# A gate sum moved from TensorE to VectorE, and linear-attention denominators computed as compact rows and spread through DRAM

## The chip, the cores and the metric

The kernel runs on one core of one Trainium2 chip. The metric is the device time in microseconds (us) of one execution, and the median of several executions is quoted. The profile's "span" is 1.5 to 2.2 us shorter than the time of the same execution, because it starts and ends with the recorded instructions.

Engines in the profile: PE is TensorE (matmuls), PEld its weight loads, DVE is VectorE, ACT is ScalarE, POOL is GpSimd, SP is SyncE, which issues most DMA transfers here.

## The reference, cut to what matters

The input x has 2048 tokens of 1024 channels; there are 32 heads of width 32; all is bf16. Branch a is linear attention with a positive feature map, branch b is dilated sliding-window attention, and a gate per token mixes them.

```python
def _A_ref(x, wqkv, wo):                       # linear attention
    ...                                        # q, k, v: [B, 32, 2048, 32]
    phi = lambda t: jnp.where(t > 0, t + 1, jnp.exp(t)) + 1e-6
    pq, pk = phi(q), phi(k)
    kv = jnp.einsum("bhsd,bhse->bhde", pk, v)
    z = jnp.einsum("bhsd->bhd", pk)
    num = jnp.einsum("bhqd,bhde->bhqe", pq, kv)
    den = jnp.einsum("bhqd,bhd->bhq", pq, z)[..., None] + 1e-6
    o = num / den
    return merge_heads(o) @ wo                 # (shortened)
...                                            # _B_ref: 8 keys per query, dilation 2
x = A_x
g = _sigmoid((x * gate_w).sum(-1, keepdims=True))
a = _A_ref(x, A_wqkv, A_wo)
b = _B_ref(x, B_wqkv, B_wo)
# result: the gated mix of a and b (g times a plus 1 - g times b)
```

Two small things in it matter here. The gate needs one sum of 1024 products per token. The denominator needs one number per head and token: 32 x 2048 numbers, each a dot product of length 32.

Of the kernel before, what the change touches and what calls it, by code (L numbers as in the profile page):

```python
# [6 lines left out]
ACT = mybir.ActivationFunctionType  # L7
ALU = mybir.AluOpType
AX = mybir.AxisListType
BF16 = mybir.dt.bfloat16  # L10
F32 = mybir.dt.float32
I32 = mybir.dt.int32

D = 1024
H = 32
# [1087 lines left out]
def build_kernel(nc, A_x, A_wqkv, A_wo, B_x, B_wqkv, B_wo, gate_w, out):  # L1103
# [10 lines left out]
    def SB(shape, dtype, name, at=None):  # L1114
        n = SZ[dtype]
        for d in shape[1:]:
            n *= d
        if at is None:
            at = base[0]
            base[0] += (n + 31) // 32 * 32  # L1120
        uid[0] += 1
        h = nc.alloc_sbuf_tensor_at("%s_%d" % (name, uid[0]), list(shape), dtype, offset=at)
        return Tile("S", h, at, list(shape), dtype)
# [32 lines left out]
    GT = [("M", 1, 2, None)]  # L1156
    gt_hbm = nc.dram_tensor("gt_hbm", [4, 512], F32)
# [16 lines left out]
    gw = SB([128, 8], BF16, "gw")  # L1174
# [3 lines left out]
    gwr = SB([128, 8, 32], BF16, "gwr")  # L1178
    kvbd = SB([128, 8, 128], BF16, "kvbd")
    zbd = SB([128, 8, 128], BF16, "zbd")  # L1180
# [9 lines left out]
    gts = SB([128, 512], F32, "gts", at=ph)  # L1190
# [8 lines left out]
    RAr = Ring([SB([128, 512], F32, "ra%d" % i, at=t.lo) for i, t in enumerate((Er.t[0], Er.t[1], Lr.t[0], vr.t[0]))])  # L1199
# [5 lines left out]
    az = Ring([SB([128, H, 33], BF16, "az%d" % i) for i in range(2)])  # L1205
    top_ = base[0]
    base[0] = ph
    osb = Ring([SB([128, 1024], BF16, "o%d" % i) for i in range(2)])
    pr = Ring([SB([128, 512], BF16, "p%d" % i) for i in range(4)])
# [14 lines left out]
    def plan(seen):  # L1224
# [25 lines left out]
        def C(eng, fn, cost, writes, reads=()):  # L1250
            return P.op(eng, fn, cost, reads=reads, writes=writes, prio=-1)
# [19 lines left out]
        C("pool", lambda e: e.memset(zbd[:], 0.0), 0.9, [zbd.all()])  # L1271
# [31 lines left out]
        def gw_load(e):  # L1303
            with nc.allow_non_contiguous_dma(reason="tiny gate_w transposed load"):
                return e.dma_start(gw[:, :], gate_w.rearrange("(dc p) -> p dc", p=128))

# [9 lines left out]
        P.op("sp", gw_load, 0.6, writes=[gw.all()], prio=20, chan="gw", lat=0.5)  # L1316
# [69 lines left out]
        P.op("dve", lambda e: e.tensor_copy(gwr[:, :, :], gw[:, :, None].to_broadcast([128, 8, 32])), 0.3, reads=[gw.all()], writes=[gwr.all()])  # L1386
        gbank = main.next()

        def gate_fn(e):
            last = None  # L1390
            for dc in range(8):
                for u in range(4):
                    last = e.matmul(gbank.ap()[32 * u:32 * u + 32, :], gwr[:, dc, :], xT[:, dc, u * 512:(u + 1) * 512], start=(dc == 0), stop=(dc == 7),  # L1393
                                    tile_position=(0, 32 * u), skip_group_check=True)
            return last
        P.op("pe", gate_fn, 1.75, mode="c", reads=[gwr.all(), xT.all()], writes=[gbank.iv], name="gate")
        P.op("act", lambda e: e.activation(gts[:, :], gbank.ap(), ACT.Exp, scale=-1.0), act(512), reads=[gbank.iv], writes=[gts.all()])
        P.op("sp", lambda e: e.dma_start(gt_hbm[:, :], gts[0:128:32, :]), 0.6, reads=[gts.all()], writes=[GT], chan="gto", lat=1.0)

        def gate_in(e):  # L1400
            with nc.allow_non_contiguous_dma(reason="2048 gates"):
                return e.dma_start(gt[:, :], gt_hbm.rearrange("u (k p) -> p (u k)", p=128))
        P.op("sp", gate_in, 0.6, reads=[GT], writes=[gt.all()], chan="gti", lat=6.0)
# [82 lines left out]
        def after(n, f, cols=False):  # L1486
            later.append((slot_n[0] + n, f, cols))
            later.sort(key=lambda x: x[0])
# [74 lines left out]
        for j in range(4):  # L1563
            sl = slice(32 * j, 32 * j + 32)
            P.op("dve", lambda e, sl=sl: e.tensor_copy(zbd[sl, :, sl], kva[sl, :, 32:33].to_broadcast([32, 8, 32])), dps(256), reads=[kva.all()], writes=[zbd.all()])
            P.op("dve", lambda e, sl=sl: e.tensor_copy(kvbd[sl, :, sl], kva[sl, :, 0:32]), 0.3, reads=[kva.all()], writes=[kvbd.all()])
# [23 lines left out]
        def numer(u, j):  # L1590
            bank = main.next()
            w, wr = w_cols(2, j)
            xs, xr = x_chunk(u)
            group(bank, w, xs, [wr, xr])
            tgt, c0 = pqn(u)
            dst, reg = tgt[:, j, c0:c0 + 512], tgt.part((j, j + 1), (c0, c0 + 512))
            if u == 0:
                p_, preg = dst, reg
            else:
                pt, _ = pr.next()  # L1600
                p_, preg = pt[:, :], pt.all()
            phi(bank, p_, preg, 8 * u + j)
            def over():
                db = main.next()
                P.op("pe", lambda e: e.matmul(db.ap(), zbd[:, j, :], p_, start=True, stop=True), mm(512), reads=[zbd.all(), preg], writes=[db.iv], name="den")  # L1605
                R, _ = RAr.next()
                P.op("act", lambda e: e.activation(R[:, :], db.ap(), ACT.Ln, bias=eps[:, :]), act(512), reads=[db.iv, eps.all()], writes=[R.all()])  # L1607
                P.op("act", lambda e: e.activation(R[:, :], R[:, :], ACT.Exp, scale=-1.0), act(512), reads=[R.all()], writes=[R.all()])  # L1608
                P.op("dve", lambda e: e.tensor_tensor(dst, p_, R[:, :], ALU.mult), 0.65, reads=[preg, R.all()], writes=[reg])
            after(6 if u == 0 else 2, over)  # L1610
# [21 lines left out]
        nums = [(u, j) for u in range(4) for j in range(8)]  # L1632
        outs = [(t, jh) for t in range(NT) for jh in range(2)]
        for n, (u, j) in enumerate(nums):
            numer(u, j)
            slot(0)
            if n == 1:
                turn()
            if 3 <= n < 11:
                fold(n - 3, 0)  # L1640
                fold(n - 3, 1)
            if n >= 17:
                a_out(*outs.pop(0))
                slot(0)
        while later:
            slot(0)
        P.op("dve", lambda e: e.tensor_reduce(mx4[:, 2:3], qe[:, :], AX.X, ALU.max), 0.2, reads=[qe.all()], writes=[mx4.part((2, 3))], prio=1e5)
        while outs:
            a_out(*outs.pop(0))


        P.op("dve", lambda e: e.tensor_scalar(mx4[:, 1:2], mx4[:, 1:2], -1.0, None, op0=ALU.mult), 0.1, reads=[mx4.part((1, 2))], writes=[mx4.part((1, 2))], prio=1e5)

        def mx_out(e):
            with nc.allow_non_contiguous_dma(reason="512 maxima"):
                return e.dma_start(mx_hbm.rearrange("i p -> p i"), mx4[:, :])
        P.op("sp", mx_out, 0.6, reads=[mx4.all()], writes=[MX], chan="mxo", lat=8.0, prio=1e5)
        P.op("sp", lambda e: e.dma_start(mxr[0:1, :, :], mx_hbm[None, :, :]), 0.1, reads=[MX], writes=[mxr.all()], chan="mxi", lat=2.0, prio=1e5)
        P.op("dve", lambda e: e.tensor_reduce(mx1[:, :], mxr[:, :, :], AX.X, ALU.max), dps(512), reads=[mxr.all()], writes=[mx1.all()], prio=1e5)
        small = [mx1.all()]  # L1660
        P.op("dve", lambda e: e.tensor_scalar(mx1[:, 2:3], mx1[:, 2:3], 2.0, None, op0=ALU.max), 0.1, reads=small, writes=small, prio=1e5)
        for o, i0, i1 in ((ALU.max, 0, 1), (ALU.mult, 0, 0), (ALU.mult, 2, 3)):
            P.op("dve", lambda e, o=o, i0=i0, i1=i1: e.tensor_tensor(mx1[:, i0:i0 + 1], mx1[:, i0:i0 + 1], mx1[:, i1:i1 + 1], o), 0.1, reads=small, writes=small, prio=1e5)
        P.op("dve", lambda e: e.tensor_scalar(mx1[:, 0:1], mx1[:, 0:1], 40.0 / DH, None, op0=ALU.is_le), 0.1, reads=small, writes=small, prio=1e5)
        P.op("dve", lambda e: e.tensor_scalar(mx1[:, 2:3], mx1[:, 2:3], 1e18 / (4 * DH), None, op0=ALU.is_le), 0.1, reads=small, writes=small, prio=1e5)
        flag_op = P.op("dve", lambda e: e.tensor_tensor(flag[:, :], mx1[:, 0:1], mx1[:, 2:3], ALU.mult), 0.1, reads=small, writes=[flag.all()], prio=1e5)


        for t in range(NT):
# [4 lines left out]
            for f0, f1 in parts:  # L1674
# [13 lines left out]
                if t == NT - 1 or f1 == 1024:  # L1688
                    c = f0 if t == NT - 1 else 0
                    P.op("sp", lambda e, e_=e_, r=r, o_=o_, c=c, f1=f1: e.dma_start(out2[e_, r * 128:(r + 1) * 128, c:f1], o_[:, c:f1]), 0.5,  # L1690
                         reads=[o_.part((c, f1))], chan="out%d_%d" % (os_, c), lat=1.0)

# [65 lines left out]
```

## The kernel before: the parts that the change and the argument touch

The kernel records its operations with their reads, writes and an assumed cost, and a small scheduler of its own lays them out for each engine and places the semaphore waits (`P.op(engine, function, assumed us, reads, writes)`). The order of each engine's list is fixed when the program is built. An instruction behind a wait comes after it.

The gate is a matmul with a one-column weight. The column is repeated 32 times, so that a 512-token chunk fills one of four column tiles. The result comes out as rows and takes a round trip through DRAM to become columns (one value per partition).

```python
P.op("dve", lambda e: e.tensor_copy(gwr[:, :, :], gw[:, :, None].to_broadcast([128, 8, 32])), ...)
def gate_fn(e):
    for dc in range(8):
        for u in range(4):
            last = e.matmul(gbank.ap()[32 * u:32 * u + 32, :], gwr[:, dc, :], xT[:, dc, u * 512:(u + 1) * 512],
                            start=(dc == 0), stop=(dc == 7), tile_position=(0, 32 * u), ...)
    return last
P.op("pe", gate_fn, 1.75, ...)
... # Exp on ScalarE, to DRAM as rows, back as columns
```

The denominators take one full matmul for each group of four heads and 512 tokens. `zbd` is block diagonal with z repeated over 32 columns, so the matmul computes each denominator 32 times, once for each of the 32 rows of its head. That is what lets the division follow without any spreading.

```python
def numer(u, j):              # u: chunk of 512 tokens, j: group of four heads
    ...                       # eight matmuls, then phi on ScalarE and VectorE -> p_
    def over():
        db = main.next()
        P.op("pe", lambda e: e.matmul(db.ap(), zbd[:, j, :], p_, start=True, stop=True), mm(512), ...)
        R, _ = RAr.next()
        P.op("act", lambda e: e.activation(R[:, :], db.ap(), ACT.Ln, bias=eps[:, :]), ...)
        P.op("act", lambda e: e.activation(R[:, :], R[:, :], ACT.Exp, scale=-1.0), ...)
        P.op("dve", lambda e: e.tensor_tensor(dst, p_, R[:, :], ALU.mult), 0.65, ...)
    after(6 if u == 0 else 2, over)
```

`after(n, f)` puts f behind n further slots. A slot is one work group of matmuls.

## Time and profile before

| | before |
|---|---|
| time, median of 3 (range) | 501.64 us (501.62 to 503.03) |
| TensorE busy | 493.2 us, 99% of the span |
| VectorE, ScalarE busy | 54%, 38% |
| gate matmuls on TensorE | 32 in 1.85 us |
| denominator matmuls on TensorE | 32, 0.216 us each, 6.9 us |
| from the end of the last computation to the end of the span | 3.9 us |

The first lines of the profile page of the kernel before give the span and each engine's busy time, its share of the span and its instructions. The third line is from the page's part on the chain that ended last: shares of the span by engine.

```profile
span 500.1 us, 11359 instructions
...
PE 493.2 (99%) x5113; PEld 231.4 (46%) x5113; DVE 267.6 (54%) x460; ACT 191.4 (38%) x331; POOL 6.6 (1%) x30
...
PE 96%; SPq 2%; DMA 1%; ACT 1%; issue 0%; DVE 0%
```

TensorE is almost never without work: its busy time (99%) and its share of the chain (96%) are the whole span but for the start and the end. Only work or waits taken from TensorE can shorten this kernel.

The groups of instructions of the kernel before, by form. The columns are: line, engine, operation, output from input, sizes, count | busy us in all, mean ns of one | idle time just before, and what ended it.

```profile
L1393 PE MATMUL ps_all<-xT,gwr 128*32 128x512 bf16 x32 | 1.9, 380 | 0.0
L1605 PE MATMUL ps_all<-p,zbd 128*128 128x512 bf16 x24 | 8.9, 379 | 0.0
L1605 PE MATMUL ps_all<-pq,zbd 128*128 128x512 bf16 x8 | 3.0, 379 | 0.0
L1607 ACT ACTIVATE ra<-ps_all,eps 128x512 f32<-128x512 f32 x32 | 21.5, 689 | 2.1 <-PE ps_all L1605 2.0
L1608 ACT ACTIVATE ra<-ra 128x512 f32<-128x512 f32 x32 | 19.9, 639 | 0.5
```

The mean of 379 ns is from the start of a matmul to its end in the record. It isn't what the matmul costs, because the next one starts 0.216 us after it, so the records overlap. The cost is read from the chain, in which matmuls follow each other. The chain of the kernel before, in order of time; the columns are start us, duration us, engine, tile, line, and count:

```profile
62.08 1.84 PE ps_all L1393 x32
...
342.17 0.23 PE ps_all L1605
342.42 0.69 ACT ra L1607
...
344.20 1.17 ACT ra L1607 x2
345.42 1.90 PE ps_all L1325 x8
...
412.71 27.63 PE ps_all L1325 x128
...
495.65 0.48 DVE o L1684
```

A full matmul costs 27.63 / 128 = 0.216 us, and a gate matmul on a quarter of the columns 1.84 / 32 = 0.058 us. At 342 the chain leaves TensorE for ScalarE: the Ln and Exp of the denominators had fallen behind, and TensorE lost about 0.4 us there. The last computation ends at 495.65 + 0.48 = 496.13.

Two readings of the kernel before. The first is the timeline at the first block of attention scores. The second is a window: stretch, its length, then busy time of TensorE, weight loads, VectorE, ScalarE and GpSimd, each with its count, then the granted clock, the share of DMA, and GB/s.

```profile
127.85 0.70 PE L1428 MATMUL ps_all<-qT,kT 32*64 32x57 bf16 x64
```

```profile
64.00:128.00 64.00, 64.00 (x328) 28.91 (x327) 34.57 (x57) 11.32 (x19) 0.00 (x0) 1.00 0.17 47
```

The gate and everything before attention lie ahead of the first of these, the denominators behind it.

### The profile page before, as it was taken

What the parts mean: (1) busy time and instruction counts of PE and PEld (TensorE: products, weight loads), DVE (VectorE), ACT (ScalarE), POOL (GpSimd) and SP (SyncE); (2) the same over time, 40 slices, a digit from 0 to 9 for tenths busy, and PEclk for the clock granted to TensorE, in tenths of its full rate; (3) what the DMA queues carried; (4) which work ended last, traced back from release to release, by engine and by line L of the source; (5) the groups of instructions that cost most, each with busy time, mean ns of one, the idle gap of its engine ahead of it and who ended that gap; (6) DMA issues with size and microseconds to landing.
All of it is one profiled execution on the core that took longest, in us unless ns stands there. A gap on an engine that the chain in (4) does not pass through costs nothing.

```text
span 500.1 us, 11359 instructions
## 1 busy us (share of the span) xinstructions
PE 493.2 (99%) x5113; PEld 231.4 (46%) x5113; DVE 267.6 (54%) x460; ACT 191.4 (38%) x331; POOL 6.6 (1%) x30
## 2 busy tenths in 40 slices
PE   8999999999999999999999999999999999999996
PEld 3444444444444445554545454444444444444443
DVE  3112136555676785665556564678776663234443
ACT  1111111111334345656655555489955543200000
POOL 5000000000000000000000000000000000000000
PEclk9999999999999999999999999999999999999999
DMA  8999990000023151011010000500000000011222
GB/s 230 202 209 312 344 283 1 1 0 1 12 90 125 32 182 34 24 42 26 27 43 24 24 1 3 171 0 1 0 2 0 1 1 0 3 43 64 84 85 67
DMA packets 47410, 34.91 MB, mean 70 GB/s; under 512 B 22261, under 2 KB 43125, under 8 KB 47354
## 3 DMA queue, kind: packets, MB, share of 16 engines
q1 hardware_dynamic: 46810, 33.59, 23.6%
q8 instruction: 42, 0.69, 0.6%
q10 hardware_dynamic: 544, 0.52, 0.4%
q14 instruction: 14, 0.11, 0.1%
HBM read 21.51 MB, written 8.40 MB: 60 GB/s over the span
## 4 chain that ended last, share of the span: by engine, by line
PE 96%; SPq 2%; DMA 1%; ACT 1%; issue 0%; DVE 0%
PE ps_all L1325 76%; PE ps_all L1680 11%; PE ps_all L1428 2%; PE ps_all L1447 2%; PE ps_all L1605 1%; SPq L1295 1%; PE ps_all L1526 1%; DMA w<-in_B_wqkv_dram 1%; PE ps_all L1454 1%; PE ps_all L1583 1%; SPq L1300 1%; ACT ra L1607 0%; PE ps_all L1393 0%; ACT e L1334 0%; ACT ra L1608 0%
## 5 line engine op out<-in xcount | busy, mean ns | idle before, releaser
L1325 PE MATMUL ps_all<-w,xT 128*128 128x512 bf16 x960 | 214.2, 379 | 1.1 <-DMA xT<-in_A_x_dram 0.9
L1325 PE MATMUL ps_all<-xT,w 128*128 128x512 bf16 x768 | 172.1, 379 | 0.1
L1325 PEld LDWEIGHTS ps_all<-w,xT 128*128 128x128 bf16 x960 | 91.1, 98 | 109.9 <-DMA w<-in_B_wqkv_dram 1.4
L1325 PEld LDWEIGHTS ps_all<-xT,w 128*128 128x128 bf16 x768 | 74.1, 98 | 88.8 <-ACT ra L1607 0.6
L1680 PE MATMUL ps_all<-w,qT 128*128 128x512 bf16 (+1 forms) x264 | 55.4, 373 | 0.0
L1680 PEld LDWEIGHTS ps_all<-w,qT 128*128 128x128 bf16 x264 | 25.8, 98 | 29.7
L1336 DVE TENSOR_SCALAR e<-e 128x512 bf16<-128x512 bf16 x64 | 18.4, 291 | 30.9 <-ACT e L1332 17.1
L1434 ACT ACTIVATE E<-ps_all 128x1824 bf16<-128x1824 f32 (+1 forms) x18 | 30.4, 1688 | 11.7 <-PE ps_all L1428 10.9
L1356 DVE CAST vst<-ps_all 128x512 bf16<-128x512 f32 x15 | 10.4, 692 | 42.7 <-PE ps_all L1325 42.7
L1437 DVE TENSOR_TENSOR E<-E,msk 128x1824 bf16<-128x1824 bf16 (+1 forms) x18 | 19.8, 1102 | 22.2 <-ACT E L1434 22.2
L1684 DVE SCALAR_TENSOR_TENSOR o<-ps_all,gm,xT 128x512 bf16<-128x512 f32 (+1 forms) x25 | 18.2, 729 | 23.0 <-PE ps_all L1680 22.8
L1334 ACT ACTIVATE e<-ps_all 128x512 bf16<-128x512 f32 x32 | 19.2, 601 | 27.5 <-PE ps_all L1325 26.0
L1332 ACT ACTIVATE e<-ps_all 128x512 bf16<-128x512 f32 x32 | 19.1, 598 | 26.7 <-PE ps_all L1325 25.8
L1281 DVE TENSOR_TENSOR mx<-mx,qT 128x1024 bf16<-128x1024 bf16 x32 | 20.7, 688 | 15.3 <-ACT qT L1360 15.2
L1281 DVE TENSOR_TENSOR mx<-mx,kT 128x1024 bf16<-128x1024 bf16 x32 | 20.7, 688 | 14.8 <-ACT kT L1357 14.7
L1357 ACT ACTIVATE vst<-ps_all 128x512 bf16<-128x512 f32 x17 | 10.2, 597 | 47.8 <-PE ps_all L1325 47.8
L1466 DVE TENSOR_TENSOR qT<-ps_all,L 128x456 bf16<-128x456 f32 (+1 forms) x36 | 21.0, 627 | 6.2 <-ACT L L1464 5.0
L1463 ACT ACTIVATE L<-ps_all 128x456 f32<-128x456 f32 (+1 forms) x36 | 17.8, 547 | 12.4 <-PE ps_all L1447 12.4
L1607 ACT ACTIVATE ra<-ps_all,eps 128x512 f32<-128x512 f32 x32 | 21.5, 689 | 2.1 <-PE ps_all L1605 2.0
L1338 DVE SCALAR_TENSOR_TENSOR pk<-ps_all,e 128x512 bf16<-128x512 f32 x32 | 21.9, 688 | 0.7
L1359 DVE TENSOR_SCALAR xT<-ps_all,g 128x512 bf16<-128x512 f32 x15 | 11.2, 750 | 19.9 <-PE ps_all L1325 19.9
L1360 ACT ACTIVATE qT<-ps_all 128x512 bf16<-128x512 f32 x14 | 8.4, 597 | 34.4 <-PE ps_all L1325 34.4
(77 smaller groups left out, 321.2 us busy)
## 6 DMA issues: line engine op xcount, KB each, us to landing
w<-in_A_wqkv_dram SPq DMA_DIRECT2D x6, 1024.0 KB, 7.0
v<-vB_hbm SPq DMA_DIRECT2D x36, 128.0 KB, 2.6
vB_hbm<-vst SPq DMA_DIRECT2D x32, 128.0 KB, 4.7
w<-in_B_wqkv_dram SPq DMA_DIRECT2D x4, 1024.0 KB, 8.4
out_dram<-o SPq DMA_DIRECT2D x15, 256.0 KB, 2.0
w<-in_A_wo_dram SPq DMA_DIRECT2D x2, 1024.0 KB, 5.2
w<-in_B_wo_dram SPq DMA_DIRECT2D x2, 1024.0 KB, 6.7
w<-in_B_wqkv_dram SPq DMA_DIRECT2D x6, 256.0 KB, 4.3
```

Source lines behind the costliest of these rows:

```text
L1281: P.op("dve", lambda e, m=m, op=op: e.tensor_tensor(m[:, 0:n], m[:, 0:n], src, op), 0.08 + n / 1920.0, reads=[m.all(), reg], writes=[m.all()],
L1325: last = e.matmul(bank.ap(), lhs(dc), rhs(dc), start=(dc == 0), stop=(dc == 7))
L1332: P.op("act", lambda e: e.activation(e_[:, :], bank.ap(), ACT.Exp), act(512), reads=[bank.iv], writes=[e_.all()])
L1334: P.op("act", lambda e: e.activation(e_[:, :], bank.ap(), ACT.Exp, accum_out=qe[:, col:col + 1]), act(512) + 0.1, reads=[bank.iv], writes= ...
L1336: P.op("dve", lambda e: e.tensor_scalar(e_[:, :], e_[:, :], 1.0, 1e-6, op0=ALU.min, op1=ALU.add), 0.25, reads=[e_.all()], writes=[e_.all()])
L1338: P.op("dve", lambda e: e.scalar_tensor_tensor(out=dst, in0=bank.ap(), scalar=0.0, in1=e_[:, :], op0=ALU.max, op1=ALU.add), dps(512), read ...
L1434: P.op("act", lambda e: e.activation(E[:, 0:32 * nq].rearrange("p (j q) -> p j q", j=4), ps[:, 4:8, 0:8 * nq], ACT.Exp), act(32 * nq), rea ...
L1437: P.op("dve", lambda e: e.tensor_tensor(ev(), ev(), m[:, :, :].rearrange("p r q -> p (r q)")[:, None, :].to_broadcast([128, 16, 2 * nq]), ...
L1466: P.op("dve", lambda e, L=L, h=h, q0=q0: e.tensor_tensor(qT[:, :, q0:q0 + nq], SO[h].ap(0, n).rearrange("p (c q) -> p c q", c=8), L[:, 0:n ...
L1607: P.op("act", lambda e: e.activation(R[:, :], db.ap(), ACT.Ln, bias=eps[:, :]), act(512), reads=[db.iv, eps.all()], writes=[R.all()])
L1680: last = e.matmul(bank.ap(0, f1 - f0), qT[:, dc, t * 128:(t + 1) * 128], ws[3][:, dc, f0:f1], start=(dc == 0), stop=(dc == 7))
L1684: P.op("dve", lambda e, bank=bank, o_=o_, t=t, n=n, i0=i0, i1=i1, tgt=tgt, c0=c0: e.scalar_tensor_tensor(out=o_[:, i0 * 128:i1 * 128].rear ...
```

## The change

The intent is to take both small things from TensorE. The gate is summed on VectorE: rows of x (tokens on partitions) are loaded once more, and one instruction multiplies them by a broadcast `gate_w` and sums along the row. The result is already a column. The denominators are computed once each and not 32 times: eight matmuls on column tiles give 32 rows for 512 tokens. Ln and Exp then run on one tile per 512 tokens instead of eight. The price is that each row must be spread over 32 partitions. That is done by storing the rows in DRAM in four copies, and loading each of these eight times.

```diff
-    zbd = SB([128, 8, 128], BF16, "zbd")
+    zsel = SB([128, 8, 32], BF16, "zsel")
-    RAr = Ring([... "ra%d" ... 4 tiles])
+    RAr = Ring([... "ra%d" ... 2 tiles])
+    RBr = Ring([SB([128, 512], F32, "rb%d" % i, at=kT.lo + 2048 * i) for i in range(12)])
+    xn = Ring([SB([128, 1024], BF16, "xn%d" % i, at=az.t[i].lo) for i in range(2)])
 ... # the gate
-        P.op("pe", gate_fn, 1.75, mode="c", ...)
-        P.op("act", ... Exp of [128, 512]); store to DRAM; load as columns
+        for t in range(NT):                                  # 16 tiles of 128 tokens
+            xt, xs_ = xn.next()
+            P.op("sp", lambda e, t=t, xt=xt: e.dma_start(xt[:, :], x2[...]), ..., chan="xn%d" % xs_)
+            P.op("dve", lambda e, t=t, xt=xt: e.scalar_tensor_tensor(out=xt[:, :], in0=xt[:, :], scalar=1.0,
+                 in1=gwb[:, :], op0=ALU.mult, op1=ALU.mult, accum_out=gt[:, t:t + 1]), dps(1024), ...)
+        P.op("act", ... Exp of gt [128, 16])
 ... # the denominators
+        def over(u):
+            db = main.next()
+            def fn(e):
+                for q in range(2):
+                    for c in range(4):
+                        last = e.matmul(db.ap()[32 * c:32 * c + 32, :], zsel[:, 2 * c + q, :],
+                                        tgt[:, 2 * c + q, c0:c0 + 512], start=(q == 0), stop=(q == 1),
+                                        tile_position=(0, 32 * c), skip_group_check=True)
+                return last
+            P.op("pe", fn, 0.55, mode="c", ...)
+            R, rs = RAr.next()
+            P.op("act", ... Ln, bias=eps);  P.op("act", ... Exp, scale=-1.0)
+            for c in range(4):
+                P.op("sp", ... e.dma_start(rc_hbm[u, 8 * c:8 * c + 8, :, :],
+                     R[32 * c:32 * c + 8, None, :].to_broadcast([8, 4, 512])), ..., chan="rco%d_%d" % (rs, c))
+            for j in range(8):
+                B, bs = RBr.next()
+                src = rc_hbm[u, 4 * j:4 * j + 4, :, :].rearrange("r k n -> (r k) n")[:, None, :].to_broadcast([16, 8, 512])
+                P.op("sp", ... e.dma_start(B[:, :], src), ..., chan="rci%d" % bs)
+                P.op("dve", lambda e, B=B, dst=dst: e.tensor_tensor(dst, dst, B[:, :], ALU.mult), 0.65, ...)
 ... # the order of work
             numer(u, j)
+            if j == 7:
+                after(3, lambda u=u: over(u))
             slot(0)
-            if n >= 17:
+            if n >= 20:
                 a_out(*outs.pop(0))
                 slot(0)
 ... # and three of the final output tiles now stand before the last eight a_out groups
```

Each new `chan` name is a further DMA channel.

## The prediction

> **What bounds the kernel now.** TensorE. The busy table has PE at 493.2 of 500.1 us (99%), VectorE 54%, ScalarE 38%. The chain of waits is 96% PE outside 10 us at the start (DMA) and 4 us at the end. In the chain the 128x512 matmuls follow each other every 0.216 us (128 in 27.63 us), at a granted clock of 1.0. So only issue slots or waits taken from PE can shorten it.
>
> **Removed from PE.** The 32 gate matmuls on four column tiles: 62.01 to 63.86 us in the timeline, 1.85 us. The 32 full-width denominator matmuls, 0.216 us each in the chain: 6.9 us.
>
> **Added to PE.** Four denominator blocks of 8 matmuls on column tiles. The gate block is the same form: 32 in 1.85 us, eight passes of 0.216 plus about 0.12 to switch. [...] So a new block is 2 x 0.216 + 0.12 = 0.55 us (estimate), four 2.2. Net: 6.9 + 1.85 - 2.2 = 6.55 us.
>
> **A wait that goes.** Between 342 and 345.5 us PE loses about 0.4 us to ScalarE, behind with Ln and Exp of the reciprocals (timeline). ScalarE loses 56 of 64 such passes, about 34 us, so it should vanish.
>
> **Moved or added elsewhere.** VectorE gets 16 products of 128x1024 with a sum; the trace has no such form, an estimate from the 128x512 form (0.69 us) is 1.2 to 1.3 us, 20 us in all. Fourteen lie between about 70 and 125 us, where VectorE is busy 34.6 of 64 us; it goes to about 80%, while PE has four banks of 1.73 us. DMA gets 4 MB of x rows, 1 MB of reciprocals written and 8 MB read. One block's spread is an estimate of 12 us: ScalarE 1.3, four stores and eight loads at about 0.5 us of issue each, two landings of about 2.5 us (v loads land in 2.6). [...] The instruction order puts ten groups or more between a block and its first reader on PE, so it is hidden. The first 62 us have DMA saturated (share 1.03), but the extra 0.75 MB there delays only loads needed later.
>
> **Predicted:** 501.64 - 6.55 - 0.4, plus 0.2 for small new waits: **494.9 us**, range 492.0 to 498.5. Faster by over 2%: 0.12; within 2%: 0.85; slower by over 2%: 0.03.
>
> **What would show it.** PE busy falls by about 7 us. The four denominator blocks take 0.5 to 0.6 us each on the chain. ScalarE busy falls from 191 to about 157 us, VectorE rises from 268 to about 287. VectorE is near 80% busy at 64 to 128 us; the chain there stays PE. Any wait of VectorE for reciprocals is under 3 us and PE doesn't notice.
>
> **What would make it wrong.** The summed product taking about 2 us, or VectorE waiting for each pair of x rows: evictions between 70 and 125 us then hold PE. A spread of over 17 us: VectorE, in order, then holds evictions in the numerator stage. The transposition of the state, one group earlier, waiting up to 1 us. A larger gain needs the removed PE work to cost more than its issue slots.

The sum: 501.64 - 6.55 - 0.4 + 0.2 = 494.9. The 0.55 us of a new block rests on the gate block alone, and the 2.5 us of a landing on the loads of v, with a median of 2.6 us on the page of the kernel before.

## More of the kernel before

The end of the program matters too. The kernel assumes that certain maxima are small, writes a flag, and behind the fast program stands a general path that the flag can choose. SyncE first waits for the last value of every DMA channel that the fast program used. Then every engine compares the flag, and normally takes a branch over the general path.

```python
def tail(e, eng):
    reg = e.alloc_register("fast_ok")
    e.wait_ge(*flag_op.val)
    e.reg_load(reg, flag[0:1, 0:1])
    if eng == "sp":
        for s, v in P.final:          # one entry for each DMA channel
            e.wait_ge(s, v)
    with e.If_eq(reg, 0):
        ...                           # general path
```

## The result, and the profile after

| | before | after |
|---|---|---|
| time, median of 4 (range) | 501.63 us (501.51 to 503.03) | 497.66 us (496.50 to 497.96) |
| ratio after / before, with 95% interval | | 0.991 [0.9887, 0.9934] |

The result is 4.0 us faster. The four executions of the kernel after lie 1.5 us apart, and the one that was profiled (497.96) is the slowest of them. A ratio, here and below, is the mean time of one kernel's runs over that of the other's runs of the same rounds, so it isn't quite the ratio of the medians quoted. The range of the prediction held, but the gain is 4.0 us where 6.7 were predicted. The rest of this document is about the missing 2.8 us.

The first lines of the profile page of the kernel after, and its chain by engine:

```profile
span 495.8 us, 11299 instructions
...
PE 479.6 (97%) x5016; PEld 228.4 (46%) x5081; DVE 275.9 (56%) x483; ACT 166.6 (34%) x287; POOL 6.3 (1%) x30
...
PE 89%; DMA 5%; issue 2%; SPq 2%; DVE 1%; ACT 1%; ACTq 0%
```

One trap comes first. TensorE's busy time seems to fall by 13.6 us, twice what was predicted. But this trace has 5016 matmuls against 5081 weight loads, where before both were 5113. The weight loads fall by exactly the 32 of the gate, so 65 matmul records are simply missing, and they leave false gaps. The waits of TensorE in the kernel after (us in all, times, longest) show it in their first line:

```profile
PE ps_all L1319 <- issue: 5.9, 37, 0.2
...
PE ps_all L1591 <- DVE xT L1332: 0.9, 1, 0.9
```

Thirty-seven gaps of 0.16 us that nothing released, inside stages that take no longer than before, are missing records. The second line is a real wait: once, for 0.9 us, TensorE stood before a denominator block (L1591), waiting for VectorE.

The groups of the kernel after that stand where those of the kernel before stood:

```profile
L1383 DVE SCALAR_TENSOR_TENSOR xn<-xn,gwb 128x1024 bf16<-128x1024 bf16 x16 | 18.9, 1221 | 0.0
L1383 DVE DVE_READ_ACCUMULATOR xn<-xn,gwb 128x1 f32 x16 | 1.4, 85 | 0.0
L1591 PE MATMUL ps_all<-xT,zsel 128*32 128x512 bf16 x24 | 1.8, 384 | 0.9 <-DVE xT L1332 0.9
L1591 PE MATMUL ps_all<-pq,zsel 128*32 128x512 bf16 x8 | 0.6, 384 | 0.0
L1607 DVE TENSOR_TENSOR xT<-xT,rb 128x512 bf16<-128x512 bf16 x24 | 16.4, 690 | 8.0 <-DMA rb<-rc_hbm 7.7
L1596 ACT ACTIVATE ra<-ps_all,eps 128x512 f32<-128x512 f32 x4 | 2.7, 684 | 4.2 <-PE ps_all L1591 4.2
```

The work is what was costed. A summed product takes 1.22 us and a read of the accumulator 0.085 us more. (The two groups of 16 show that each summed product is two instructions on VectorE.) The denominators take 2.4 us of TensorE in place of 6.9. ScalarE does Ln four times in place of 32. (The 6.9 is the cost on the chain. The busy time of 8.9 + 3.0 us in the groups of the kernel before counts each matmul to the end of its record.)

The same two readings of the first part as before, from the timeline and the windows of the kernel after:

```profile
125.66 0.70 PE L1411 MATMUL ps_all<-qT,kT 32*64 32x57 bf16 x64
```

```profile
62.00:126.00 64.00, 63.68 (x335) 29.01 (x339) 48.01 (x82) 13.50 (x24) 0.48 (x2) 1.00 0.40 127
```

The attention begins 2.19 us earlier. VectorE is busy 48.0 of 64 us in the stage that now holds the sums, not 34.6, and TensorE doesn't notice.

The chain of the kernel after, in order of time, around the denominators and at the end. The DMA issues below it give output from input, queue, kind, count, KB each, and median us from issue to landing.

```profile
339.07 3.38 DMA rc_hbm<-ra
...
346.81 6.43 DMA rb<-rc_hbm
353.26 0.69 DVE pq L1607
...
358.14 3.31 DMA rc_hbm<-ra
...
365.42 5.84 DMA rb<-rc_hbm
371.27 0.69 DVE xT L1607
371.97 0.61 DVE xT L1332
372.62 0.62 PE ps_all L1591 x8
373.24 6.15 PE ps_all L1319 x28
...
489.74 0.48 DVE o L1644
```

```profile
rb<-rc_hbm SPq DMA_DIRECT2D x32, 256.0 KB, 5.2
...
xn<-in_A_x_dram SPq DMA_DIRECT2D x16, 256.0 KB, 2.7
out_dram<-o SPq DMA_DIRECT2D x15, 256.0 KB, 2.1
```

This chain is the wait of 0.9 us, read backwards. The third denominator block starts at 372.62, because the phi of its last input on VectorE (L1332) ran at 371.97. That phi stood in VectorE's order behind a multiplication by reciprocals (L1607), and this multiplication waited for a load from DRAM which had been on its way since 365.42. The loads of x, 256 KB each and issued by SyncE, have a median of 2.7 us from issue to landing, and the outputs one of 2.1. The loads of reciprocals have the same size and a median of 5.2. But they come eight in a row: they were issued 0.7 us apart and landed about 1.0 us apart (the first of a row after 3.7 to 3.9 us, the last after up to 6.4), and in the midst of a row the DMA engines were fully busy, as this window of the kernel after shows (the share of DMA is the last but one number, 1.00):

```profile
346.00:350.00 4.00, 3.95 (x20) 1.80 (x19) 2.99 (x6) 1.38 (x4) 0.00 (x0) 1.00 1.00 264
```

A median of 5.2 us instead of the predicted 2.5 is where the wait begins.

Where the time went, stage by stage, from these records:

| stretch of the profiled runs | before | after | gain | predicted |
|---|---|---|---|---|
| start to first block of attention scores | 127.85 | 125.66 | 2.19 | 1.85 |
| from there to the end of the last VectorE operation | 368.28 | 364.57 | 3.71 | 5.1 |
| from there to the end of the span | 3.94 | 5.56 | -1.62 | 0 |
| sum | 500.07 | 495.79 | 4.28 | 6.75 (net of 0.2) |

(5.1 is 6.9 - 2.2 + 0.4.) About 1.4 us are missing in the middle and 1.6 us at the very end, where the change has edited nothing.

The last stretch holds no computation, so the page says little about it. The records of SyncE in the trace were read one by one for the following table; it isn't a view of the profile page. "Walk" is from the end of SyncE's last issue of an output to its branch over the general path: it contains a load of the flag (0.5 us) and the waits for all DMA channels. "Gap" is from the branch to SyncE's next instruction, which stands behind the general path.

| | SyncE instructions up to the branch | wait instructions in the walk | walk, us | gap, us | last VectorE operation to end of span, us |
|---|---|---|---|---|---|
| before | 157 | 26 | 2.21 | 0.51 | 3.94 |
| after | 229 | 36 | 3.25 | 1.08 | 5.56 |

The 53 DMA channels before have become 73, chiefly through the new rings (`rco`, `rci`, `xn`). One wait instruction carries up to two waits (each of the 36 records of the kernel after has two semaphores). So ten more wait instructions stand in the walk, which is 1.0 us longer, and the gap behind it is 0.6 us longer. By the same records the last output had landed 0.2 us before the branch in the kernel before, but 1.55 us before it in the kernel after: there SyncE is no longer waiting for data. Wait instructions follow each other every 0.061 us, so ten more are 0.6 us. Most of the other 0.4 us is one pause between two waits (0.40 us from the one to the next). It stands between SyncE's 207th and 208th instruction in all four kernels with the new denominators and 36 waits, whichever wait that is. Its cause is open.

The windows of the kernel after also say that the clock is not part of it. It is 1.00 up to 490 us, and its mean of 0.996 comes from the last slices alone, with no matmul in them. One of them:

```profile
492.00:494.00 2.00, 0.00 (x0) 0.00 (x0) 0.00 (x0) 0.00 (x0) 0.00 (x0) 0.50 0.08 19
```

### The profile page after: what moved, and what is told of

Read it like the earlier page. It is cut to its first block, busy times and chain, and to the rows that moved or that the text cites. A ratio compares the mean times of both kernels' runs of the same rounds, so it can differ in the third digit from the quotient of the medians.

```text
span 495.8 us, 11299 instructions
## 1 busy us (share of the span) xinstructions
PE 479.6 (97%) x5016; PEld 228.4 (46%) x5081; DVE 275.9 (56%) x483; ACT 166.6 (34%) x287; POOL 6.3 (1%) x30
## 4 chain that ended last, share of the span: by engine, by line
PE 89%; DMA 5%; issue 2%; SPq 2%; DVE 1%; ACT 1%; ACTq 0%
PE ps_all L1319 71%; PE ps_all L1640 11%; DMA rb<-rc_hbm 2%; PE ps_all L1411 2%; PE ps_all L1430 2%; SPq L1604 2%; DMA rc_hbm<-ra 1%; PE ps_all L1509 1%; DMA xT<-in_A_x_dram 1%; PE ps_all L1437 1%; DVE xT L1332 1%; PE ps_all L1567 1%; DVE pq L1607 0%; PE ps_all L1591 0%; DVE e L1330 0%
## 5 line engine op out<-in xcount | busy, mean ns | idle before, releaser
L1319 PE MATMUL ps_all<-w,xT 128*128 128x512 bf16 x923 | 207.4, 380 | 5.3 <-issue 4.4
L1319 PE MATMUL ps_all<-xT,w 128*128 128x512 bf16 x748 | 168.5, 379 | 2.1 <-issue 1.4
L1332 DVE SCALAR_TENSOR_TENSOR pk<-ps_all,e 128x512 bf16<-128x512 f32 x32 | 21.9, 688 | 0.7
L1351 ACT ACTIVATE kT<-ps_all 128x512 bf16<-128x512 f32 x16 | 9.6, 598 | 35.8 <-PE ps_all L1319 35.8
L1607 DVE TENSOR_TENSOR xT<-xT,rb 128x512 bf16<-128x512 bf16 x24 | 16.4, 690 | 8.0 <-DMA rb<-rc_hbm 7.7
L1354 ACT ACTIVATE qT<-ps_all 128x512 bf16<-128x512 f32 x16 | 9.6, 598 | 31.4 <-PE ps_all L1319 31.4
```

The costliest lines, as they stand in the source:

```text
L1319: last = e.matmul(bank.ap(), lhs(dc), rhs(dc), start=(dc == 0), stop=(dc == 7))
L1332: P.op("dve", lambda e: e.scalar_tensor_tensor(out=dst, in0=bank.ap(), scalar=0.0, in1=e_[:, :], op0=ALU.max, op1=ALU.add), dps(512), read ...
L1351: fa = lambda e: e.activation(dst, src(), ACT.Copy)
```

## The experiments

The theory had two parts. First, about 0.9 us is the single wait of the third block, which comes from its place in the order and from the slow loads of reciprocals. Second, about 1.6 us is the end of the program: SyncE walks through waits that have long been satisfied, one after the other, for as many channels as the program has ever used. There were these rivals: the middle loss comes from VectorE being loaded with the gate; the end loss is the landing of the last output, and the walk lies under it; the gap is hidden by a longer walk, and grows when the walk is shorter. The expectations name their theories by letters; each says what it means. Ten kernels ran, all with right results, each beside the kernel before on the same chip.

| kernel | median us | before, same rounds | ratio [95%] |
|---|---|---|---|
| gate part only | 500.19 | 501.80 | 0.9969 [0.9956, 0.9982] |
| denominator part only | 500.67 | 501.68 | 0.9981 [0.9967, 0.9995] |
| after, third block two slots later | 496.68 | 501.80 | 0.9897 [0.9883, 0.9911] |
| after, walk over output channels alone | 498.62 | 501.80 | 0.9936 [0.9920, 0.9952] |
| both of these | 497.15 | 501.91 | 0.9902 [0.9885, 0.9919] |
| before, with 20 more waits | 502.77 | 501.80 | 1.0028 [1.0015, 1.0041] |
| after, one copy in DRAM | 519.90 | 501.68 | 1.0377 [1.0360, 1.0394] |
| after, third block later and waits earlier | 494.79 | 501.68 | 0.9864 [0.9849, 0.9879] |
| before, waits earlier | 501.43 | 501.68 | 0.9995 [0.9982, 1.0009] |
| third block later, half of the waits | 495.11 | 501.91 | 0.9862 [0.9845, 0.9878] |

And the end of each, from SyncE's records as above:

| kernel | SyncE instructions up to the branch | waits in the walk | walk | gap | last VectorE operation ends | from there to the end |
|---|---|---|---|---|---|---|
| before | 157 | 26 | 2.21 | 0.51 | 496.13 | 3.94 |
| after | 229 | 36 | 3.25 | 1.08 | 490.23 | 5.56 |
| gate part only | 171 | 26 | 2.20 | 0.51 | 493.87 | 3.99 |
| denominator part only | 215 | 36 | 3.23 | 1.88 | 492.14 | 6.30 |
| third block later | 229 | 36 | 3.24 | 1.02 | 489.57 | 5.41 |
| walk over outputs alone | 195 | 2 | 2.26 | 2.77 | 490.61 | 6.20 |
| both of these | 195 | 2 | 1.86 | 2.93 | 489.83 | 5.99 |
| before, 20 more waits | 167 | 36 | 2.98 | 0.51 | 496.31 | 4.64 |
| one copy in DRAM | 229 | 36 | 3.24 | 1.01 | 512.19 | 5.33 |
| third block later, waits earlier | 230 | 2 | 1.95 | 0.51 | 489.55 | 3.54 |
| before, waits earlier | 158 | 2 | 1.88 | 0.51 | 496.15 | 3.56 |
| third block later, half of the waits | 212 | 2 | 1.77 | 0.51 | 489.60 | 3.67 |

### The gate part alone

Edit: the kernel after, with the denominators, the order of work and the buffers of before.

```diff
 # gate: as after (xn, gwb, sum on VectorE)
-    zsel, RBr, rc_hbm, over(u), three early output tiles
+    zbd, pr, over() inside numer(u, j), order as before
```

> The kernel before with only the gate's sum moved to VectorE (denominators as before; 26 wait instructions at the end, as before). Theory A (PE loses the gate's 1.85 us of issue slots and nothing waits for VectorE or the x rows): about 499.8 us, 1.7 to 2.2 us faster than before, VectorE busy up by 19 to 21 us. Rival B (VectorE at 80 to 90% in the k and q stage, or the x rows in the busy DMA stage, holds PE): less than 1.2 us faster, with PE waits between 62 and 128 us.

Measured: 500.19 us, 1.6 us better than before. The last VectorE operation ends 2.26 us earlier, the end is as before (3.99). The window of the stage is the same as in the kernel after:

```profile
62.00:126.00 64.00, 63.68 (x343) 29.08 (x347) 48.01 (x82) 13.55 (x24) 0.48 (x2) 1.00 0.40 131
```

The 1.6 us are just short of the 1.7 to 2.2 expected, with executions 1.0 us apart; the profiled one was the fastest of its five. After the start, no wait of TensorE for VectorE or for the added rows of x stands in the trace. So the gate part does what was predicted of it, and no cost of its own is seen.

### The denominator part alone

Edit: the kernel after, with the gate of before.

```diff
-        for t in range(NT): ... scalar_tensor_tensor(... accum_out=gt[:, t:t + 1])
+        P.op("pe", gate_fn, 1.75, mode="c", ...)   # and the round trip through DRAM
 # denominators: as after
```

> The changed kernel with the gate back on TensorE as in the kernel before: only the denominators are changed. Theory A (the two parts are independent and add up): 1.6 to 2.2 us slower than the changed kernel, so about 499.5 us, with a wait of about 1 us before the third denominator block as in the changed kernel. Rival B (the gate's VectorE work is what makes VectorE late in the numerator stage): the wait before the third block goes and the time is under 498.5 us.

Measured: 500.67 us, only 1.0 us better than before and 1.2 us slower than expected; the gap at its end is 0.8 us longer than in the kernel after. Up to the last VectorE operation the gain is 3.99 us, of which the end takes back 2.4 (6.30 instead of 3.94). The wait before the third block is there without any of the gate's work. Its wait of TensorE, and its window of the early stage, in which VectorE is back at 34.9 us:

```profile
PE ps_all L1609 <- DVE xT L1339: 0.9, 1, 0.9
```

```profile
64.00:128.00 64.00, 64.00 (x356) 29.12 (x355) 34.88 (x58) 11.00 (x19) 0.00 (x0) 1.00 0.17 47
```

This refutes the rival that blamed the gate's load on VectorE. The two parts add up as far as the last computation: 2.26 + 3.99 = 6.25 us against 5.90 of the whole change. Their ends don't add up, and both losses belong to the denominator part.

### The third block two slots later

Edit on the kernel after:

```diff
             if j == 7:
-                after(3, lambda u=u: over(u))
+                after(3 if u != 2 else 5, lambda u=u: over(u))
```

The `3` counts slots. From `n` = 20 on, each round has two slots, because an `a_out` group is put in between. In TensorE's order, read from the trace, two groups of matmuls stand between the last numerator group of its tokens and the third block, where the second block has four. (The first has two as well, and two pairs of folding matmuls, but no reciprocals hold up VectorE yet.)

> The changed kernel with the third denominator block (tokens 1024 to 1535) two work groups later in PE's order. Theory A (the block stands only two groups behind the last phi of its tokens, and VectorE, held up by reciprocals not yet landed, is late with that phi): the wait of 1.1 us before this block goes, and the time falls by 0.8 to 1.2 us, to about 496.7 us. Rival B (VectorE itself is the limit of this stage): the wait moves to another PE instruction in the same stage and the time stays within 0.4 us of 497.7 us.

Measured: 496.68 us, where the kernel after had 497.66 (in other rounds; ratios to before 0.9897 and 0.991, whose intervals overlap, so the gain in time alone is not clear of the noise). What shows the effect is the trace. The chain of this kernel at the same place:

```profile
369.07 6.42 PE ps_all L1319 x29
375.49 0.55 PE ps_all L1591 x8
376.04 2.70 PE ps_all L1319 x12
```

The block now follows the matmuls before it without a gap and takes 0.55 us. The middle stretch is 0.91 us shorter (364.57 to 363.66 us), which is the wait. This part of the theory is shown. What is left of the middle loss is 0.5 us: the four blocks took 0.62, 0.63, 0.55 and about 0.6 us in the kernel after where 0.55 was assumed, which is 0.2, and the rest was not traced further.

### The walk over the output channels alone

Edit on the kernel after. The transfers of the other channels have readers that wait for them.

```diff
+        self.last = [(self.csem[c], n) for c, n in chan_n.items() if c.startswith('out')]
...
         if eng == "sp":
-            for s, v in P.final:
+            for s, v in P.last:
                 e.wait_ge(s, v)
```

> The changed kernel, but at the end SyncE waits only for the four output channels instead of for all DMA channels (2 wait instructions instead of 36). Theory A (the end of the changed kernel is longer because SyncE walks through ten more wait instructions after the last output was issued): the stretch from the end of the last VectorE instruction to the end of the span falls from 5.6 us to 3.5 to 4.2 us, and the time by 1.4 to 2.0 us, to about 496 us. Rival B (the outputs land later, because other transfers are still under way): the stretch stays at 5 us or more, and the time at 497.7 us.

Measured: 498.62 us, where about 496 was expected. By the medians it is 1 us slower than the kernel after; the intervals of the two ratios overlap, so it is safe to say only that nothing was gained. The miss is instructive. The walk did get shorter by 1.0 us (3.25 to 2.26), but the gap behind the branch rose from 1.08 to 2.77 us. The theory of the walk alone was not enough; the branch needed attention as well.

### Both of these together

```diff
-                after(3, lambda u=u: over(u))
+                after(3 if u != 2 else 5, lambda u=u: over(u))
-            for s, v in P.final:
+            for s, v in P.last:
```

> The changed kernel with the third denominator block two groups later and the waits for all channels but the outputs left out altogether, so it differs from the run with the waits moved ahead only by 34 wait instructions fewer, far from the end. Theory A (the gap after SyncE's last branch depends on where the branch and its target lie in SyncE's program): the gap is near 2.8 us as in the run that left the waits out of the changed kernel, and the time is 496.5 to 498 us. Rival B (that gap is chance of a run, or came from other causes): gap near 0.5 to 1 us and time near 494.8 us.

Measured: 497.15 us, so no better than the later third block alone (496.68; the intervals overlap). The walk is 1.86 us and the gap 2.93. The long gap of the previous run was no accident of one build.

### The kernel before, with twenty more waits

```diff
-            for s, v in P.final:
+            for s, v in P.final + P.final[:20]:
                 e.wait_ge(s, v)
```

> The kernel before with twenty more waits at the end of SyncE's program, for DMA channels that finished long ago (36 wait instructions instead of 26, as in the changed kernel). Theory A (the walk through wait instructions sets the end): 1.1 to 1.6 us longer than before, about 503.0 us, all of it after the last VectorE instruction. Rival B (waits for channels long finished cost nothing that shows): 501.6 us, no change.

Measured: 502.77 us against 501.80, ratio 1.0028 (1.4 us) with an interval that leaves 1 out; the medians differ by 0.97 us. Expected were 1.1 to 1.6. Ten more wait instructions, all long satisfied, make the walk 0.77 us longer: 0.6 us by their spacing of 0.061 us, the rest mostly a pause of 0.2 us between two of them. That refutes the rival under which the walk lies wholly under the landing of the last output. With two wait instructions, in the later runs, the walk is 1.8 to 2.3 us, which is then the landing of the last output: in all five such kernels the branch follows this landing by 0.1 us. With 26 it is hardly longer (2.21 us); with 36 it is 3.0 to 3.25, of which 0.6 us over 26 waits are the waits themselves and 0.2 to 0.4 the pause. The gap stays at 0.51 us.

### One copy in DRAM instead of four

Edit on the kernel after: each row is stored once and read 32 times, where four copies were read eight times each. The bytes loaded are the same.

```diff
-    rc_hbm = nc.dram_tensor("rc_hbm", [4, H, 4, 512], F32)
+    rc_hbm = nc.dram_tensor("rc_hbm", [4, H, 1, 512], F32)
-                     R[...].to_broadcast([8, 4, 512])
+                     R[...].to_broadcast([8, 1, 512])
-                     [:, None, :].to_broadcast([16, 8, 512])
+                     [:, None, :].to_broadcast([4, 32, 512])
```

> The changed kernel with the reciprocals written to DRAM once instead of four times, and each row read 32 times instead of each of four copies 8 times. Theory A (the time from issue to landing of the reads is set by the amount read and by issue, not by how many copies stand in DRAM): the reads still land in 4.5 to 6 us, VectorE waits 8 to 12 us for them as in the changed kernel, and the time is within 0.4 us of 497.7 us. Rival B (many reads of one row queue up behind each other): landings over 7 us and at least 0.6 us slower.

Measured: 519.9 us, 22 us slower than the kernel after. The waits of TensorE and VectorE in this kernel:

```profile
PE ps_all L1591 <- DVE xT L1332: 14.1, 2, 7.1
```

```profile
DVE xT L1607 <- DMA rb<-rc_hbm: 36.9, 22, 1.9
...
DVE pq L1607 <- DMA rb<-rc_hbm: 11.2, 8, 1.9
```

VectorE waits 48 us for reciprocals, as the multiplications of a block come one every 2.57 us in the timeline (358.71, 361.28, 363.83), and TensorE waits 14 us before two denominator blocks and 3 us at another place. After each of these three waits its granted clock was 0.5 for 3 to 5 us more (until 367.87, 391.77 and 422.49 us). In the chain at that clock, the block at 388.55 took 1.07 us where the one at 422.93 took 0.55, and the eight matmuls from 419.64, at that clock for 2.85 us, took 3.29 us where eight took 1.73 before. So these stretches, 11.2 us in all, cost it another 5.6 us (an estimate: half of that time). Together this is about the 22 us.

Within 0.4 us of the kernel after had been expected, so this is a large miss. It doesn't show, though, that reading one DRAM row often is slow, because the edit changed a second thing: the outermost dimension of the load's source went from 16 to 4. The window of one block's loads in this kernel, to be compared with the one of the kernel after above (share of DMA 1.00, 264 GB/s):

```profile
372.00:388.00 16.00, 9.41 (x44) 4.05 (x42) 7.36 (x14) 2.75 (x7) 0.00 (x0) 0.90 0.26 101
```

A share of 0.26 is about that of four of the 16 DMA engines that the profile counts (4/16 = 0.25, an estimate). Other records fit it. Each load here reports its end by 5 semaphore updates and not by 16; the stores of reciprocals, with 8 outermost, report by 9, and the loads of x, with 128, by 16. And the packets of 2 KB took 0.084 us here (median), the same as those of the loads of x in the kernel after, so these reads of one row 32 times were not slower. (Those of the reciprocals in the kernel after took 0.10 to 0.13, with all engines busy.) That the loads were slow because few engines carried them is the author's reading of these records. No run with one copy and 16 outermost was made, so it is not shown by an experiment. What the run does confirm is the shape of the first part of the theory: a slow spread reaches TensorE through the phi that stands behind the multiplications in VectorE's order.

### The third block later, and the waits made before the last outputs

The idea after the miss above: leave the program as long as it was, but do the walk while SyncE has nothing else to do. The waits for all channels but the outputs now stand before the last ten operations of SyncE, and the tail waits for the outputs alone. Edit on the kernel with the later third block:

```diff
         def run(e, eng):
-            for o, waits in plan[eng]:
+            last = len(plan[eng]) - 10
+            for i, (o, waits) in enumerate(plan[eng]):
+                if eng == "sp" and i == last:
+                    for c, n in chan_n.items():
+                        if not c.startswith("out"):
+                            e.wait_ge(self.csem[c], n)
...
-            for s, v in P.final:
+            for s, v in P.last:
```

> The changed kernel with the third denominator block two groups later, and with the waits for all channels but the outputs moved ahead of the last ten outputs in SyncE's program, where it has idle time; the number of instructions is the same. Theory A (the walk through the waits after the last output issue costs about 1 us[...]): branch reached 0.7 to 1.1 us earlier after the last VectorE instruction than in the changed kernel, the gap after the branch stays near 1 us, time 495.6 to 496.1 us. Rival B (the gap after the branch grows whenever the walk is shorter[...]): the gap grows to 2 us or more, and the time stays at 496.5 us or more.

Measured: 494.79 us, the best of all, and 0.9864 of the time before. It beats both kernels, and the 495.6 to 496.1 us that were expected, because the gap fell too, which nothing had predicted. The walk is 1.95 us, the gap 0.51, the whole end 3.54 us. Its profile page has complete records of matmuls (as many as weight loads), so that TensorE's true busy time can be read:

```profile
span 493.1 us, 11365 instructions
...
PE 486.8 (99%) x5081; PEld 228.1 (46%) x5081; DVE 274.5 (56%) x481; ACT 167.9 (34%) x289; POOL 6.3 (1%) x30
```

493.2 - 486.8 = 6.4 us were taken from TensorE, where 6.55 were predicted. No wait of TensorE for VectorE is left in it after the start.

### The kernel before, with the waits made earlier

The same edit of the tail on the kernel before.

> The kernel before with its waits for all channels but the outputs moved ahead of the last ten outputs in the same way. Theory A (in the kernel before the walk of 26 wait instructions ended about when the last output landed, so it cost little): within 0.5 us of 501.8 us[...]. Rival B[...]: the gap after the branch grows from 0.5 us to 2 us or more, and the time rises by 0.8 us or more.

```diff
+                if eng == "sp" and i == last:      # as above
+                    for c, n in chan_n.items(): ...
-            for s, v in P.final:
+            for s, v in P.last:
```

Measured: 501.43 us against 501.68, a ratio of 0.9995 whose interval holds 1. So the early waits are worth nothing clear of the noise in the kernel before (0.4 us at the end of the trace), and 1.9 us in the other (496.68 to 494.79, and 5.41 to 3.54 us at the end). Of these 1.9 us, 1.3 are the walk and 0.5 the gap, which is luck as long as its cause is open. What they mend is what the change broke. Between this kernel and the previous one, measured in the same rounds with the same tail, lie 501.43 - 494.79 = 6.64 us: the gain that had been predicted, 6.7.

The gap is 0.51 us here with a short walk. Under the rival that a long walk hides the gap behind the branch, it would be long.

### The third block later, with half of the waits early

To see what sets the gap: the same as the best kernel, but with only some channels waited for early, so that SyncE's program has 212 instructions and not 230. (Channels that are neither in this half nor outputs are not waited for at the end at all.)

```diff
-                        if not c.startswith("out"):
+                        if not c.startswith("out") and c[0] in "xvg":
                             e.wait_ge(self.csem[c], n)
```

> As the run with the waits moved ahead, but only about half of them stand there, so that SyncE's branch lies 18 instructions earlier. Theory A (the gap after the branch depends on its place in the program): a gap between 0.5 and 2.8 us that need not be 0.5, likely 1.5 us or more, as the other two programs of 195 and 215 instructions had 2.8 and 1.9 us. Rival B (with the walk away from the end the gap is 0.5 us wherever the branch lies): 0.5 us and 494.8 us.

Measured: 495.11 us (ratio 0.9862, so the same as the best within its scatter), with a gap of 0.51 us, where the first theory in that text expected likely 1.5 or more. Length of program alone doesn't order the gaps: with 157, 158, 167, 171, 212 and 230 instructions it is 0.51 us; with 195, 2.8 and 2.9; with 215, 1.9; with 229, 1.0 to 1.1. Kernels of the same length agree, which speaks for a property of the build and against chance.

What sets the gap stays open. In the two kernels with the longest gaps, packets of the instruction queues fall between SyncE's branch and its next instruction (at 493.4 and 493.8 us in one of them), but in the three with 1.0 to 1.1 us none does, and in one with 0.51 us one does. The records don't say for which engine a packet is. Between 171 and 230 instructions the gap isn't monotone, and no run varied the position of the branch alone, so no cause is shown. VectorE, ScalarE and GpSimd have a gap too after the same branch: 2.45 to 3.14 us in the traces of the kernels before and after. There it is hidden: in the kernel after, VectorE's next instruction comes at 493.17 us and SyncE's at 495.51.

## Why the prediction was right or wrong, point by point

- **TensorE as what bounds the kernel.** Right. All the gain is work taken from TensorE.
- **6.55 us net taken from TensorE.** Right: 6.4 us in the trace with complete records. The start to the attention gained 2.19 (1.85 predicted). The other 0.3 is likely not the gate's work: TensorE's waits for DMA at the start were 0.9 us in the kernel before and 0.4 in the kernel after.
- **"So a new block is 2 x 0.216 + 0.12 = 0.55 us."** Nearly right: 0.55 to 0.63 us, four of them 0.2 over the sum. The trace of the kernel after has the two passes and a longer step at both ends: in the second block the four matmuls of a pass start within 0.01 us of each other, the second pass starts 0.226 us after the first, and the steps from the full matmul before and to the one behind are 0.31 us each instead of 0.216.
- **The wait for ScalarE that goes.** Right: no wait of TensorE for Ln or Exp stands in the kernel after. ScalarE's busy time fell to 166.6 and not 157 us, and VectorE's rose to 275.9 and not 287. The scheduler gives copies marked for any engine to the freer one, and ScalarE, made free, took over copies that VectorE had done. Neither figure matters to the time.
- **"1.2 to 1.3 us for a summed product"**, and VectorE near 80% in that stage with PE unmoved: right (1.22 + 0.085 us; 48.0 of 64 us is 75%).
- **"Two landings of about 2.5 us ... so it is hidden."** This step failed. The loads of reciprocals landed in 5.2 us, and the spread, from ScalarE's first instruction to the last landing, took 15.4 to 16.4 us where 12 were estimated. The estimate let the eight loads follow each other at 0.5 us of issue (the issue of a load of v took 0.445 us in the median in the kernel before; that of a load of reciprocals took 0.598 in the kernel after); they landed about 1.0 us apart, with the DMA engines fully busy. VectorE's longest wait for them was 2.6 us, within what was foreseen, but "PE doesn't notice" was wrong: once it did, for 0.9 us. The prediction counted ten groups between a block and its first reader on TensorE. It didn't count that VectorE, in order, holds back the phi which the next block needs, and that the third block stood only two groups behind its last phi. The prediction named this very mechanism as a danger, but for spreads of over 17 us (its estimate; ten groups of 1.73 us are 17.3); 16.0 (the second block's) were enough.
- **"plus 0.2 for small new waits."** This is the term that was mis-sized. It measured 0.9 us for the wait of the third block, about 0.5 us of smaller losses in the same stretch, and 1.6 us at the end. The end was in no term at all: the prediction never asked what twenty new DMA channels cost in the tail, where SyncE waits for each one. The walk explains 1.0 of the 1.6 us, shown by twenty waits added to the kernel before and by early waits in the kernel after: 0.6 are the ten wait instructions, and most of the rest is the pause between two of them. The other 0.6 is the gap behind the branch. The causes of the pause and of the gap are open.

In sum, predicted 494.9, measured 497.66. With one number changed for the wait, and the waits moved off the end, 494.79 was measured. That this is so near the prediction is in part luck, as the gap shrank with the same edit.

## What to carry to other kernels

When a change adds DMA channels or semaphores, read the code that runs after the last computation as well: here each wait instruction, already satisfied, cost 0.061 us once the walk outlasted the landing of the last output, and making the waits earlier, with the same third block, took the walk from 3.24 to 1.95 us. When work is sent on a detour through DRAM, ask not only when its result is needed, but what stands behind it in the order of the engine that waits for it (here a phi, and behind it 0.9 us of TensorE). When an edit changes the shape of a transfer, look at the share of the DMA engines that it keeps busy (here 0.26 against 1.00) before explaining its time by anything else. And in these twelve builds the gap behind one branch was 0.51 to 2.93 us, with no cause shown, so compare two builds by stretches, up to the last computation and from there on, before giving a difference to the edit.
